# Joined small products per chunk on TensorE and a written-out order in the opening of an attention and two-MoE kernel

## The chip, the cores and the metric

The kernel runs on one core of a Trainium2 chip. Its engines work side by side and wait for each other by semaphores: TensorE multiplies matrices (its products and its weight loads are two rows of a profile, PE and PEld), VectorE (DVE), ScalarE (ACT) and GpSimd (POOL) work on elements, and SyncE (SP) issues most transfers. What counts is the device time of one execution in microseconds, lower is better.

## The reference

A gated linear attention over 4 sequences of 768 tokens (8 heads of 48) feeds a dense gated layer over 3072 tokens, whose result feeds a layer of 8 experts of which each token takes the best one.

```python
f = 1.0 / (1.0 + np.exp(-f_logit))
for t in range(S):
    state = f[:, :, t, :, None] * state + np.einsum('bhd,bhe->bhde', k[:, :, t], v[:, :, t])
    y[:, :, t] = np.einsum('bhd,bhde->bhe', q[:, :, t], state)
...
gate = 1.0 / (1.0 + np.exp(-(x @ w_gate)))
val = x @ w_val
x = gate * val @ w_out
...
logits = x @ moe2_w_gate              # one of 8 experts for a token, by argmax
h = np.maximum(np.einsum('ecd,edf->ecf', disp, w1), 0.0)
out = gate_w * np.einsum('ecf,efd->ecd', h, w2)
```

The weights of the dense layer arrive as 64-bit numbers and are turned into pairs of 32-bit ones (a high and a low part) on the chip.

## The kernel before

The 3072 tokens are 24 chunks of 128. A chunk's attention is done in stages, each a function `s...(i)`: s0a to s0c make the decays (transposes of the gate's logits on TensorE, a tanh on ScalarE, two scans on VectorE), s1 and s1b turn keys and queries and scale them, s2 makes the scores of the eight heads (L425), s2b masks them on VectorE (L435), s3 turns the scaled keys back (L443), s4 makes the chunk's own state, kn times v (L456), and s4b adds it to the state before (`u`, L477). s4a multiplies the state by the decays on GpSimd into `up` (L466), in which a mask leaves only a head's own 48 by 48 block of each pair of heads. The order of chunks is `SEQ`: the first chunks of the first three sequences come first, so chunks 0 to 2 and 18 have no earlier state. Chunks 7, 12, 17 and 23 are the last of their sequences and make no state (no s3, no s4).

The output is made in one of two ways. Chunks 0 to 5 (`SPLIT_FROM` is 6) have s5: tokens on rows, L488 for the earlier state and L496 for the own scores, with v or `up` moving; a copy; and s6 and s6b, which turn the result with TensorE (L517) and split it into xh and xl (L526, L527). Chunks 6 to 23 have s5t: columns on rows, L542 for the scores with v stationary, and L553 for the earlier state, in which each head uses its own rows r of `up` and of the queries. Its result is copied (L565), stored to DRAM by s6t as `xt` (L574), read back as `x` (L576) in the arrangement of the next layer, and split by s6x (L587, L588).

The dense layer goes over 8 blocks of 3 chunks. A block has 12 steps of 27 products with 384 or 392 moving columns: g1 (L756) makes gate and value, g1b the nonlinearity, and g2 (L789) adds into three output banks, which evac copies out after a block's last step. While block n runs, the chunks of block n + 1 are done between its products: `STEPS` says which stage stands in which of eight half-steps of a chunk (for chunks 3 to 5 a list in `chunk`). So chunks 3 to 5 are done in block 0.

Before block 0 stands the opening: the list `EARLY` of stages for chunks 0 to 2 and parts of 3, with `W` for a step of the weights' conversion. Such a step works on several units of weights at once: three VectorE instructions convert one unit (L637, L645, L652), ScalarE and VectorE split the one before (L718, L719), and an output unit is turned on TensorE (L715), copied (L725) and multiplied by the experts' gate (L736). 36 units are converted in all, in the opening and in block 0. In the program before, only SyncE's instructions keep the written order; on the other engines a scheduler moves them ahead of each other by its own estimates. The code around the change that sets the opening's order is this:

```python
for item in EARLY.split():
    if item == "W":
        weights_step()
    else:
        i, stage = item.split(".")
        stages[stage](int(i))
```

Of the kernel before, what the change touches and what calls it, by code (L numbers as in the profile page):

```python
# [8 lines left out]
F32 = mybir.dt.float32  # L9
# [23 lines left out]
STEPS = "s1b s3 +lq;;s2 s2b;s4 s4b;+s0a;s5t +s0b;s6t +s0c *lv +s4a;s6x +s1"  # L33

EARLY = """
0.s0a 0.s0b W 0.s0c W 0.s1 0.s1b W 1.s0a 1.s0b W 0.s3 1.s1 0.s2 0.s4 1.s0c W 2.lq 1.s1b
W 2.s0a 1.s2 0.s2b 2.lv 0.s4b 2.s0b W 0.s5 2.s0c 1.s3 1.s2b W 2.s1 2.s1b 1.s4 1.s4b 2.s3 3.lv 4.lq
1.s5 3.lq W 2.s2 0.s6 0.s6b W 3.s0a 2.s2b 1.s6 3.s0b W 1.s6b 2.s4 2.s4b 2.s5 W 2.s6 4.lv 3.s0c 2.s6b
# [3 lines left out]
EARLY_BANKS = ("a0", "a1", "a2", "acc0", "acc1", "pv")  # L42
# [23 lines left out]
def kernel(  # L66
# [197 lines left out]


# [215 lines left out]

    def s5(i):
        b, c = SEQ[i]
        y = att_bank()
        qt, vt = C[i]["qt"], v_t.pop(i)
        for p in range(NPAIR):
            if c > 0:
                nc.tensor.matmul(  # L488
                    y[:, p * 2 * D : (p + 1) * 2 * D],
                    lhsT=qt[0:PR, p * P : (p + 1) * P],  # L490
                    rhs=C[i]["up"][:, p, :],
                    start=True,
                    stop=False,
                )
            for h in (2 * p, 2 * p + 1):
# [1195 lines left out]
```

## Time and profile before

| what | before |
|---|---|
| device time, median of 3 runs (range) | 888.56 us (887.03 to 888.79) |
| the profiled execution, its time | 888.59 us |
| its span, first to last instruction | 886.8 us |
| TensorE products busy | 856.0 us, 97% |
| TensorE weight loads busy | 814.6 us, 92% |
| VectorE busy | 528.2 us, 60% |
| ScalarE busy | 396.5 us, 45% |
| GpSimd busy | 188.6 us, 21% |
| mean granted clock of TensorE | 0.982 |

A share of busy time is a mean over stages with different limits. The page of the profile also cuts the span into 40 slices: VectorE is nine tenths busy or nearly so in slices 2 to 6 and five to seven tenths in most of those after, and TensorE's granted clock is below full in the first slices alone. So the opening is read apart from the rest, by stretches. TensorE's busy time has a model in it (products overlap and their ends are worked out), so the time of a group of products is read from starts, not from busy times.

### The profile page before, as it was taken

How to read it: one execution, taken by the hardware profiler on the slowest of the kernel's cores; microseconds unless marked ns; L12 is line 12 of the kernel's file. 1: busy time of each engine (PE TensorE's matmuls, PEld its weight loads, DVE VectorE, ACT ScalarE, POOL GpSimd, SP SyncE). 2: the span in 40 equal slices, each digit the busy share in tenths (PEclk: the TensorE clock that was granted, in tenths of full speed). 3: DMA queues.
4: the chain of work that ended last, by engine and by line, in shares of the span. 5: the costliest groups of instructions: out<-in, count | busy, mean ns of one | idle time of the engine just before them, and what ended most of it. 6: DMA issues, size and time to landing. Idle time of an engine off the chain costs nothing.

```text
span 886.8 us, 15168 instructions
## 1 busy us (share of the span) xinstructions
PE 856.0 (97%) x5627; PEld 814.6 (92%) x5627; DVE 528.2 (60%) x1227; ACT 396.5 (45%) x972; POOL 188.6 (21%) x249
## 2 busy tenths in 40 slices
PE   4999999999999999999999999999999999999995
PEld 4889989999999999999999999999899999999995
DVE  5889997756755765665675663353765525644521
ACT  3544433555554554544445454332455525543521
POOL 2032210121111111110110110020274225423311
PEclk8789999999999999999999999999999999999998
DMA  9756543543543533423544441130457235335000
GB/s 224 149 141 154 153 112 82 134 113 96 155 112 78 151 97 99 126 80 105 138 107 108 126 109 54 63 141 21 168 171 249 70 131 195 100 113 172 26 22 25
DMA packets 130245, 103.54 MB, mean 117 GB/s; under 512 B 52056, under 2 KB 123272, under 8 KB 130162
## 3 DMA queue, kind: packets, MB, share of 16 engines
q1 hardware_dynamic: 126546, 93.04, 38.0%
q0 software_dynamic: 3616, 9.44, 3.2%
q8 instruction: 46, 0.75, 0.4%
q14 instruction: 37, 0.30, 0.1%
HBM read 89.95 MB, written 13.46 MB: 117 GB/s over the span
## 4 chain that ended last, share of the span: by engine, by line
PE 79%; DVE 10%; issue 5%; ACT 1%; POOL 1%; DMA 1%; SPq 0%; POOLq 0%; DVEq 0%; ACTq 0%
PE acc L789 16%; PE pv L756 16%; PE pg L756 16%; PE acc L1168 6%; PE pg L1147 5%; PE pv L1147 4%; PE a L425 2%; PE acc L1183 2%; PE a L542 2%; PE a L553 2%; PE a L456 1%; DVE a L652 1%; DVE a L645 1%; PE a L1126 1%; POOL out_dram L1225 1%
## 5 line engine op out<-in xcount | busy, mean ns | idle before, releaser
L768 DVE SCALAR_TENSOR_TENSOR th<-th,pv 128x384 f32<-128x384 f32 x96 | 52.6, 548 | 110.7 <-PE pv L756 109.0
L756 PE MATMUL pg<-xh,wh 128*128 128x384 f32 x288 | 102.3, 355 | 1.2 <-ACT th L766 0.6
L789 PE MATMUL acc<-oh,hh 128*128 128x392 f32 x288 | 101.4, 352 | 0.3 <-ACT x L818 0.3
L789 PE MATMUL acc<-ol,hh 128*128 128x392 f32 x288 | 98.5, 342 | 0.0
L756 PE MATMUL pg<-xl,wh 128*128 128x384 f32 x288 | 97.7, 339 | 0.8 <-DVE xl L527 0.8
L756 PE MATMUL pv<-xh,wh 128*128 128x384 f32 x288 | 97.5, 339 | 0.8 <-DVE th L768 0.7
L756 PE MATMUL pg<-xh,wl 128*128 128x384 f32 x288 | 97.7, 339 | 0.0
L789 PE MATMUL acc<-oh,hl 128*128 128x392 f32 x288 | 97.7, 340 | 0.0
L756 PE MATMUL pv<-xh,wl 128*128 128x384 f32 x288 | 97.0, 337 | 0.0
L756 PE MATMUL pv<-xl,wh 128*128 128x384 f32 x288 | 96.5, 335 | 0.0
L766 ACT ACTIVATE th<-pg 128x384 f32<-128x384 f32 x96 | 47.1, 491 | 100.5 <-PE pg L756 98.2
L773 ACT CAST hh<-th 128x384 fp32r<-128x384 f32 x96 | 49.2, 513 | 94.1 <-DVE th L768 92.3
L466 POOL TENSOR_TENSOR up<-u,gm 112x384 f32<-112x384 f32 x20 | 36.5, 1824 | 213.7 <-PE a L553 189.1
L774 DVE TENSOR_TENSOR hl<-th,hh 128x384 fp32r<-128x384 f32 x96 | 54.0, 562 | 36.8 <-ACT hh L773 36.8
L674 ACT ACTIVATE piece<-piece,tiny 128x192 f32<-128x192 f32 x144 | 67.4, 470 | 17.4 <-DMA piece<-in_moe_w_val_dram 6.3
L756 PEld LDWEIGHTS pg<-xh,wh 128*128 128x128 f32 x288 | 54.4, 189 | 5.4 <-issue 3.3
L789 PEld LDWEIGHTS acc<-oh,hh 128*128 128x128 f32 x288 | 54.0, 188 | 2.8 <-ACT x L818 0.6
L756 PEld LDWEIGHTS pv<-xh,wh 128*128 128x128 f32 x288 | 54.3, 189 | 2.1 <-DVE th L768 1.6
L756 PEld LDWEIGHTS pg<-xl,wh 128*128 128x128 f32 x288 | 54.6, 190 | 1.3 <-DVE xl L527 1.2
L756 PEld LDWEIGHTS pg<-xh,wl 128*128 128x128 f32 x288 | 54.5, 189 | 0.0
L789 PEld LDWEIGHTS acc<-ol,hh 128*128 128x128 f32 x288 | 54.2, 188 | 0.1
L756 PEld LDWEIGHTS pv<-xl,wh 128*128 128x128 f32 x288 | 54.3, 189 | 0.0
(335 smaller groups left out, 2051.2 us busy)
## 6 DMA issues: line engine op xcount, KB each, us to landing
r<-in_moe_w_dram SPq DMA_DIRECT2D x16, 1536.0 KB, 7.6
raw<-in_moe_w_out_dram SPq DMA_DIRECT2D x12, 384.0 KB, 4.0
raw<-in_moe_w_gate_dram SPq DMA_DIRECT2D x12, 384.0 KB, 3.8
raw<-in_moe_w_val_dram SPq DMA_DIRECT2D x12, 384.0 KB, 3.6
v<-in_v_dram SPq DMA_DIRECT2D x24, 192.0 KB, 3.3
x1d<-x SPq DMA_DIRECT2D x24, 192.0 KB, 1.9
piece<-in_moe_w_gate_dram SPq DMA_DIRECT2D x24, 192.0 KB, 3.4
piece<-in_moe_w_val_dram SPq DMA_DIRECT2D x24, 192.0 KB, 3.1
```

The costliest lines, as they stand in the source:

```text
L425: nc.tensor.matmul(pair(sc[hh], p), lhsT=pair(kt, p)[r0 : r0 + D], rhs=pair(qt, p)[r0 : r0 + D], start=True, stop=True)
L466: nc.gpsimd.tensor_tensor(out=up, in0=state[b], in1=gm_t.pop(i)[0:PR], op=ALU.mult)
L542: nc.tensor.matmul(pair(y, p)[64 * z : 64 * z + D], lhsT=vt[:, h * D : (h + 1) * D], rhs=C[i]["a", z][:, p, :], start=(p == 0), stop=(c == ...
L674: nc.scalar.activation(out=words[:, :, 0], in_=words[:, :, 1], func=AF.Sign, bias=tiny[:, z : z + 1], accum_out=above[:, z, n % NF : n % N ...
L756: nc.tensor.matmul(ps[:, 0:nt], lhsT=w[:, kk, :], rhs=x[:, kk, 0:nt], start=(m == 0), stop=(m == len(ops) - 1))
L766: nc.scalar.activation(out=th[:, 0:nt], in_=pg[:, 0:nt], func=AF.Tanh, scale=0.5)
L768: nc.vector.scalar_tensor_tensor(out=g[:, 0:nt], in0=th[:, 0:nt], scalar=1.0, in1=pv[:, 0:nt], op0=ALU.add, op1=ALU.mult)
L773: nc.scalar.copy(out=hh[:, 0:nt], in_=g[:, 0:nt])
L774: nc.vector.tensor_tensor(out=hl[:, 0:nt], in0=g[:, 0:nt], in1=hh[:, 0:nt], op=ALU.subtract)
L789: nc.tensor.matmul(acc[i][:, 0:DE], lhsT=a[:, ts], rhs=w, start=(f == 0 and m == 0), stop=(f == NF - 1 and m == 2),)
L1147: nc.tensor.matmul(ps, lhsT=wt[:, kk, fs], rhs=x[:, kk, c0 : c0 + w], start=(m == 0), stop=(m == len(ops) - 1))
L1168: nc.tensor.matmul(acc[e, d][:, 0 : CAPS[e]], lhsT=w[:, f, d * P : (d + 1) * P], rhs=a[:, 0 : CAPS[e]], start=(f == 0 and m == 0), stop=(f ...
```

## The change

The state group s4 makes two products of a pair of heads in place of one: 64 and 48 stationary columns, 48 moving ones, each to its own half of the result's rows. So only a head's own block is made, `u` is half as large, and `up` is made with all 112 rows of a pair for each head (the mask's zeros stand in the other head's rows). L553's successor takes all these rows. GpSimd makes a second product, `uc`, the decayed state without the mask's zeros, which s4b adds. In `STEPS` s3 moves to the half-step of s2, and s4 and s4b to that of s5t. s5, s6 and s6b are gone: all chunks use s5t, s6t and s6x. s6t is cut in two: it stores, and the new s6i reads back; for chunks 0 to 2 the store is issued by ScalarE. In the opening the instructions of TensorE and ScalarE keep the written order too, `EARLY` is written anew, and `warm` puts products of the identity by itself (256 columns, in bank pv, read by nobody) at the start (12) and at each `X` (8).

```diff
-STEPS = "s1b s3 +lq;;s2 s2b;s4 s4b;+s0a;s5t +s0b;s6t +s0c *lv +s4a;s6x +s1"
+STEPS = "s1b +lq;;s3 s2 s2b;;+s0a;s4 s4b s5t +s0b;s6t s6i +s0c *lv +s4a;s6x +s1"
 EARLY = """
-...
-1.s5 3.lq W 2.s2 0.s6 0.s6b W 3.s0a 2.s2b 1.s6 3.s0b W 1.s6b 2.s4 2.s4b 2.s5 W 2.s6 4.lv 3.s0c 2.s6b
+0.s0a X 0.s0b W 0.s0c 0.s1 X W 0.s1b W 1.s0a X 1.s0b W 0.s3 0.s2 1.s1 0.s4 1.s0c W 2.lq 1.s1b
+W 2.s0a 0.s2b 1.s2 0.s4b 2.s0b W 0.s5t 0.s6t 2.lv 2.s0c 1.s3 1.s2b W 2.s1 2.s1b 1.s4 1.s4b 2.s3 1.s5t 1.s6t 3.lv 4.lq
+3.lq 0.s6i W 2.s2 0.s6x W 3.s0a 2.s2b 3.s0b W 1.s6i 1.s6x 2.s4 2.s4b 2.s5t 2.s6t 4.lv W 3.s0c 2.s6i 2.s6x
 3.s4a
 """
-EARLY_BANKS = ("a0", "a1", "a2", "acc0", "acc1", "pv")
+EARLY_BANKS = ("a0", "a1", "a2", "acc0", "acc1")
+WARM = (12, 8)
...
+    def warm(n):
+        w = ident.bitcast(BF16)
+        for _ in range(n):
+            nc.tensor.matmul(bank("pv")[:, 0 : 2 * P], lhsT=w[:, 0:P], rhs=w, start=True, stop=True)
...
         for p in range(NPAIR):
-            ps = slice(p * 2 * D, (p + 1) * 2 * D)
-            nc.tensor.matmul(
-                kv[0:PR, ps], lhsT=kn[:, p * PR : (p + 1) * PR], rhs=vt[:, ps], start=True, stop=True
-            )
+            for z in range(2):
+                h, n = 2 * p + z, (64, D)[z]
+                nc.tensor.matmul(
+                    kv[64 * z : 64 * z + n, p * D : (p + 1) * D],
+                    lhsT=kn[:, p * PR + 64 * z : p * PR + 64 * z + n],
+                    rhs=vt[:, h * D : (h + 1) * D],
...
-            nc.gpsimd.tensor_tensor(out=up, in0=state[b], in1=gm_t.pop(i)[0:PR], op=ALU.mult)
+            nc.gpsimd.tensor_tensor(
+                out=up,
+                in0=state[b].unsqueeze(2).to_broadcast([PR, NPAIR, 2, D]),
+                in1=gm_t.pop(i)[0:PR].rearrange("p a (z d) -> p a z d", z=2),
+                op=ALU.mult,
+            )
+            uc = atp.tile([PR, NPAIR, D], F32, tag="uc", name="uc")
+            nc.gpsimd.tensor_tensor(
+                out=uc,
+                in0=state[b],
+                in1=e_all[0:PR, i, :].unsqueeze(2).to_broadcast([PR, NPAIR, D]),
+                op=ALU.mult,
+            )
...
-                r = slice(64 * z, 64 * z + D)
                 nc.tensor.matmul(
-                    pair(y, p)[r],
-                    lhsT=C[i]["up"][r, p, z * D : (z + 1) * D],
-                    rhs=pair(qt, p)[r],
+                    pair(y, p)[64 * z : 64 * z + D],
+                    lhsT=C[i]["up"][:, p, z],
+                    rhs=pair(qt, p)[0:PR],
...
-            nc.sync.dma_start(out=rows_[z], in_=t[64 * z : 64 * z + D])
-        x = at2["pool"].tile([P, KD, P], F32, tag="x", name="x", bufs=2)
-        nc.sync.dma_start(out=x, in_=d.rearrange("(k p) t -> p k t", p=P))
+            (nc.scalar if i < len(blocks[0]) else nc.sync).dma_start(out=rows_[z], in_=t[64 * z : 64 * z + D])
+        C[i]["d"] = d
+
+    def s6i(i):
+        if i < len(blocks[0]):
+            x = com.tile([P, KD, P], F32, tag="th", name="x")
...
+        nc.sync.dma_start(out=x, in_=C[i].pop("d").rearrange("(k p) t -> p k t", p=P))
...
+        with tc.manual_schedule(engines={mybir.EngineType.SP, mybir.EngineType.PE, mybir.EngineType.Activation}):
+            warm(WARM[0])
+            for item in EARLY.split():
+                if item == "W":
+                    weights_step()
+                elif item == "X":
+                    warm(WARM[1])
+                else:
+                    i, stage = item.split(".")
+                    stages[stage](int(i))
```

On TensorE, in a chunk of the later blocks, the state group stands between block products before (L456, `kn` and `v` into a bank `a`; L789 and L756 are the block's products):

```order
L789 MATMUL acc_1797<-oh_724,hh 128x392
L789 MATMUL acc_1797<-ol_725,hh 128x392
L789 MATMUL acc_1797<-oh_724,hl 128x392
L456 MATMUL a_2302<-v,kn 112x96 x4
L756 MATMUL pg<-xh,wh_1310 128x384
L756 MATMUL pg<-xl,wh_1310 128x384
```

Of the change, the same engine between the last product into a block's banks (L777) and the next block product (L744):

```order
L777 MATMUL acc_1921<-oh_261,hl 128x392
L466 MATMUL a_1925<-v,kn 64x48
L466 MATMUL a_1925<-v,kn 48x48
...
L522 MATMUL a_1936<-a_1850,v 48x128
L522 MATMUL a_1936<-a_1852,v 48x128
...
L532 MATMUL a_1936<-qt,up 48x128 x8
L744 MATMUL pg<-xh,wh_688 128x384
```

The state group has moved from a place of its own to directly ahead of the output group, and no block product stands between them.

On ScalarE, at the end of the opening, before: `ysb` and `xh` of chunk 2 and what stands around them (`u` is a chunk's state, `oh` and `wh` are the high parts of weights, `wot` the copy of a turned output unit).

```order
L479 COPY u_571<-a2_566 112x384
L718 CAST oh5_550<-a_506 128x384
L725 COPY wot_562<-pg_552 128x384
L505 COPY ysb_582<-acc0_573 128x384
L526 CAST xh_492<-acc1_600 128x3x128
L718 CAST wh7_592<-a_548 128x384
```

Of the change, the same engine from the weight cast ahead of chunk 1's `xh` to chunk 2's `xh` (`t` is chunk 2's output, `xt` its store):

```order
L706 CAST wh8_766<-a_686 128x384
L575 CAST xh_584<-x_648 128x3x128
L506 COPY u_661<-acc1_652 112x192
L545 COPY t_672<-a0_663 48x512 x2
L554 DMA xt_675<-t_672 48x4x128 x2
L706 CAST wh7_688<-a_632 128x384
...
L713 COPY wot_831<-a0_821 128x384
L575 CAST xh_584<-x_702 128x3x128
```

The cast of a weight now stands ahead of chunk 1's `xh`, chunk 2's output goes through two copies and two stores, and its `xh` comes eight rows later.

## Rows read from the trace of the kernel before

**Rows 1.** Busy time by stretch: stretch, length, each engine's us, TensorE's clock, DMA.

```profile
8.10:46.40 38.30, 31.59 (x208) 28.70 (x208) 32.80 (x74) 18.52 (x41) 0.92 (x3) 0.78 0.90 189
53.30:150.30 97.00, 94.48 (x628) 89.61 (x629) 84.71 (x179) 38.33 (x80) 17.99 (x20) 0.98 0.46 121
150.30:560.00 409.70, 409.31 (x2936) 389.26 (x2935) 252.45 (x585) 205.89 (x551) 59.23 (x73) 1.00 0.41 110
```

**Rows 2.** TensorE's waits from 130 to 640: for whom, total us, times, longest.

```profile
PE acc L1183 <- DVE hl L1153: 1.3, 1, 1.3
```

**Rows 3.** Timeline of TensorE from 330 to 370: start, us, line, tiles, shapes, count.

```profile
337.66 0.93 PE L456 MATMUL a<-v,kn 128*112 128x96 f32 x8
...
338.64 0.34 PE L756 MATMUL pg<-xl,wh 128*128 128x384 f32 x1
...
343.04 0.34 PE L789 MATMUL acc<-oh,hl 128*128 128x392 f32 x1
343.30 1.08 PE L542 MATMUL a<-a,v 128*48 128x128 f32 x16
344.31 1.08 PE L553 MATMUL a<-qt,up 48*48 48x128 f32 x16
...
345.60 0.33 PE L756 MATMUL pg<-xl,wh 128*128 128x384 f32 x1
...
353.32 0.55 PE L443 MATMUL a<-ident,kt 112*128 112x112 f32 x4
...
353.90 0.34 PE L789 MATMUL acc<-ol,hh 128*128 128x392 f32 x1
```

**Rows 4.** TensorE's waits from 0 to 160, the two longest.

```profile
PE pg L715 <- DVE a L652: 4.5, 1, 4.5
PE a L344 <- DMA xf<-in_f_logit_dram: 4.1, 1, 4.1
```

**Rows 5.** Timeline of TensorE around chunk 5's output, in block 0.

```profile
129.23 0.36 PE L488 MATMUL a<-up,qt 112*128 112x96 f32 x2
...
132.09 0.33 PE L756 MATMUL pv<-xl,wh 128*128 128x384 f32 x1
...
133.48 0.49 PE L517 MATMUL a<-ident,ysb 128*128 128x128 f32 x3
...
133.99 0.34 PE L789 MATMUL acc<-ol,hh 128*128 128x392 f32 x1
```

**Rows 6.** Timeline of TensorE in the opening, two scores of one pair of heads.

```profile
19.18 0.42 PE L425 MATMUL a<-qt,kt 48*128 48x128 f32 x1
19.22 0.42 PE L425 MATMUL acc<-qt,kt 48*128 48x128 f32 x1
```

**Rows 7.** Timeline at the opening's end: last mask of chunk 2, first block products.

```profile
45.74 0.69 DVE L435 TENSOR_TENSOR a<-acc,mask 128x512 f32<-128x512 f32 x1
...
49.93 0.59 PE L756 MATMUL pg<-xh,wh 128*128 128x384 f32 x1 [0.57 <-ACT xh L526]
...
53.32 0.69 PE L756 MATMUL pg<-xl,wh 128*128 128x384 f32 x1 [0.78 <-DVE xl L527]
```

**Rows 8.** The tiles t and x (ns min/median/max; landing in us), and one issue.

```profile
L565 ACT COPY t<-a x36: 560/582/583, 157.4 to 559.0; 48x512 f32<-48x512 f32 x36
L574 SPq DMA_DIRECT2D xt<-t x36: 309/310/437, 158.0 to 559.6; - x36
DMA to landing us min/median/max: 1.9/1.9/2.1
DMA to landing us min/median/max: 1.8/2.6/4.2
6.55 2.77 SPq L276 DMA_DIRECT2D xk<-in_k_dram  x1
```

**Rows 9.** Timeline of TensorE: four transposes of keys, early and in block 0.

```profile
10.43 1.06 PE L400 MATMUL acc<-ident,xk 128*128 128x128 f32 x4
...
87.82 0.65 PE L400 MATMUL a<-ident,xk 128*128 128x128 f32 x4
```

More of the change, by code (lines that the diff above doesn't have):

```diff
@@ L454, in s4 @@
         for p in range(NPAIR):
-            ps = slice(p * 2 * D, (p + 1) * 2 * D)
-            nc.tensor.matmul(
-                kv[0:PR, ps], lhsT=kn[:, p * PR : (p + 1) * PR], rhs=vt[:, ps], start=True, stop=True
-            )
+            for z in range(2):
[4 more added lines that the diff above has]
+                    rhs=vt[:, h * D : (h + 1) * D],
+                    start=True,
+                    stop=True,
+                )
         C[i]["kv"] = kv
@@ L480, in s4b @@
         state[b] = u
[L482 to L495, printed above, removed]
-                nc.tensor.matmul(
-                    y[:, h * D : (h + 1) * D],
-                    lhsT=C[i]["a", h % 2][:, p, :],
-                    rhs=vt[:, h * D : (h + 1) * D],
-                    start=(c == 0),
-                    stop=(c == 0 or h % 2 == 1),
-                )
-        pool, tag = (com, "th") if i < len(blocks[0]) else (atp, "kn")
-        ysb = pool.tile([P, DM], F32, tag=tag, name="ysb")
-        nc.scalar.copy(out=ysb, in_=y[:, 0:DM])
-        C[i]["ysb"] = ysb
-    def s6(i):
-        n = next(n for n, b in enumerate(blocks) if i in b)
-        j = blocks[n].index(i)
-        if j == 0:
-            xh_t[n] = xp.tile([P, KD, MAXB * P], F32R, tag="xh", name="xh")
-            xl_t[n] = xp.tile([P, KD, MAXB * P], F32R, tag="xl", name="xl")
-        ysb = C[i].pop("ysb")
-        yt = att_bank()
-        for kk in range(KD):
-            nc.tensor.transpose(yt[:, kk * P : (kk + 1) * P], ysb[:, kk * P : (kk + 1) * P], ident)
-        C[i]["yt"] = yt
-    def s6b(i):
-        n = next(n for n, b in enumerate(blocks) if i in b)
-        j = blocks[n].index(i)
-        yt = C[i].pop("yt")
-        src = yt[:, 0:DM].rearrange("p (k t) -> p k t", k=KD)
-        xh, xl = xh_t[n][:, :, j * P : (j + 1) * P], xl_t[n][:, :, j * P : (j + 1) * P]
-        nc.scalar.copy(out=xh, in_=src)
-        nc.vector.tensor_tensor(out=xl, in0=src, in1=xh, op=ALU.subtract)
     at2 = {}
@@ L560, in s5t @@
                 )
-        t = at2["pool"].tile([P, NPAIR, P], F32, tag="t", name="t", bufs=2)
+        pool, bufs = (atp, 1) if i < SPLIT_FROM else (at2["pool"], 2)
+        t = pool.tile([P, NPAIR, P], F32, tag="t", name="t", bufs=bufs)
         src = y.rearrange("p (a t) -> p a t", a=NPAIR)
@@ L1287, in chunk @@
                 [(s0a, n)] if nx else [],
-                [(s2, i), (s2b, i)] + ([(s0b, n)] if nx else []),
-                [(s3, i), (partial(then, load_qk), i)] + ([(s0c, n)] if nx else []),
-                [(s4, i), (s4b, i)],
-                [(s5, i)],
-                [(s6, i), (s6b, i), (load_v, i + 2)],
-                [(s4a, n)] if nx else [],
+                [(s3, i), (s2, i), (s2b, i)] + ([(s0b, n)] if nx else []),
+                [(partial(then, load_qk), i)] + ([(s0c, n)] if nx else []),
+                [(s4, i), (s4b, i), (s5t, i)],
+                [(s6t, i), (load_v, i + 2)],
+                [(s6i, i)],
+                [(s6x, i)] + ([(s4a, n)] if nx else []),
             ]
         stages = dict(s4a=s4a, s0a=s0a, s0b=s0b, s0c=s0c, s1=s1, s1b=s1b, s2=s2, s2b=s2b, s3=s3, s4=s4, s4b=s4b)
-        stages.update(s5t=s5t, s6t=s6t, s6x=s6x, s5=s5, s6=s6, s6b=s6b, lq=load_qk, lv=load_v)
+        stages.update(s5t=s5t, s6t=s6t, s6i=s6i, s6x=s6x, lq=load_qk, lv=load_v)
         plan = {}
```

25 lines of the change are left out of this document (11 added, 14 removed).

## The prediction

> **What bounds the kernel now.** I first read which engine is busy in each stretch. From 150.3 to 560 us TensorE is busy 409.31 of 409.70 us at a clock of 1.00 [rows 1], and between 130 and 640 us its longest wait is 1.3 us [rows 2]. There the kernel is a queue of products, and whatever a chunk's small products take from that queue is time of the kernel, one for one. The opening is different. From 8.1 to 46.4 us, between the first weights' arrival and the end of chunk 2's masks, VectorE works 32.80 of 38.30 us while TensorE runs at a mean clock of 0.78 [rows 1]: VectorE's queue sets the pace, with 5.5 us of waits in it. From 53.3 us, when block 0's products start in earnest, to 150.3 us, when block 0 is evacuated, TensorE is busy 94.48 of 97.00 us [rows 1, 7]. So the change has three terms: the chunks' groups in the steady part, the products of chunks 3 to 5 inside block 0, and the moment at which block 0 starts.
>
> **The steady groups.** One product of 384 columns starts 0.174 us after the one before it, one of 392 columns 0.177 us. What a group takes is the time to the second block product behind it, less those steps. The state group (s4) starts at 337.66 and the second product behind it at 338.64: 0.98 - 0.17 = 0.81 us. The output group (L542 and L553) follows a product that started at 343.04, and the second product behind it starts at 345.60: 2.56 - 0.35 = 2.21 us. The transposes (s3) run from 353.32 to 353.90: 0.58 - 0.18 = 0.40 us [rows 3]. Entering the output group takes 0.26 us instead of 0.18. L542's 16 instructions start 0.054 us apart (its 1.08 us end 0.27 us, one instruction's length, after the last start), so the seventeenth could start at 344.16; L553, which uses other rows of the array, starts at 344.31 [rows 3]. With all 112 rows of `up` the change puts L553's successor on the same half-width columns as L542, so I let this 0.15 us go. The new state group uses those columns too and stands directly ahead. Entering, 16 starts of the state group, 32 of 0.054 and 0.42 to the second block product (344.31 + 16 x 0.054 to 345.60) make 0.26 + 16p + 1.73 + 0.42, less 0.35: 2.06 + 16p us, against 0.81 + 2.21 = 3.02 before.
>
> The price p of one instruction of the new state group stands in no row: there are twice as many, with 64 or 48 stationary columns instead of 112 and 48 moving instead of 96. From above, L542 with 128 moving columns starts every 0.054; from below, two such products that use different halves start 0.04 us apart at the low clock (19.18 and 19.22) [rows 3, 6], and half of 0.054 is 0.027. The old state group's 8 instructions end after 0.93 us, a start each 0.096 us for 112 stationary columns [rows 3], which is 0.048 for a mean of 56. I take 0.048, the row of the same operation. A chunk then takes 2.83 instead of 3.02: 0.19 us less; with 0.027 it is 0.53, with 0.054 0.10.
>
> The Trainium skill (TensorE: Matmul & The Clock Gate, Wait — 56ns, not 53.3ns?) speaks of about 62 ns for every product when its instructions are decoded in the sequencer's code. By that the group would be 16 x 0.062 = 0.99 us, an estimate, and the join would lose 0.03 us a chunk. The starts 0.04 us apart [rows 6] speak against it here.
>
> Transposes and scores (s3, s2) are joined as well. Alone, s3 pays some 0.09 us on its return to block products; joined, the scores wait at s3's end for the array to change its division, about as long. I count nothing, and cover the term by 0 to 0.1. Of chunks 6 to 23, 13 have a state group and an earlier state: 13 x 0.19 = 2.5 us. Four last chunks have no state group and gain the 0.15: 0.6. Chunk 18 gains some 0.15. **Steady term: -3.2 us**, from 0 (a start each 0.06) to -7.7.
>
> GpSimd's new product `uc` is half as large as `up`, and VectorE's sum is halved. Neither is on the path: from one chunk's state to the next chunk's use there are eight half-steps, some 24 us. If that cover were gone, 1 us a chunk would show.
>
> **Chunks 3 to 5.** Their output was made from 129.23 to the second product at 132.09, 2.86 - 0.17 = 2.69 us, and turned by s6 in 133.99 - 133.48 - 0.18 = 0.33 us [rows 5]. With a state group of 0.8 that is 3.8; now 2.8. **-3.0 us** for three chunks, all in the stretch in which TensorE is busy. Their trip through DRAM has half a block to end in.
>
> **The opening.** In the new queue of VectorE eight instructions fewer stand ahead of chunk 2's last mask: one conversion of three, two splits, the first xl, small ones not counted; by 0.55 to 0.4 us each with their overlap some 2.8 us. 32.8 - 2.8 = 30.0 us of work from 8.1: the masks end at 38.1 + s, where s is what VectorE still waits. Before, chunk 2's output, its transposes and xh followed at once, and the first block product came at 49.93, 3.5 us behind the masks' end [rows 7]. Now the way is longer. ScalarE's queue has the cast of a weight (wh8_766) ahead of chunk 2's copies, and this weight's conversion stands 22 instructions behind the mask on VectorE: by their shapes some 8.5 us. Then come the cast, chunk 1's xh and the copy of u, 0.5 us each; two copies of 0.58; two DMA issues of 0.31; 1.9 us to landing; another issue; 2.6 us for x; and xh, 0.5 [rows 8]. These make 1.5 + 1.2 + 0.6 + 1.9 + 0.4 + 2.6 + 0.5 = 8.7 us. Block 0 starts at 38.1 + 8.5 + 8.7 + s = 55.3 + s. For s I take half of the 5.5 us of before, 2.7: the idle-time products and the written order bring chunk 0 forward, but TensorE still has holes and will not keep its clock. **Start at 58.0 instead of 53.3**, between 55.3 and 62 (twice the old half where both queues wait for each other).
>
> The 36 idle-time products cost 256/384 of 0.174, 0.116 us each at the high clock, 0.23 at the low: 4 to 8 us in all, where TensorE waited 4.1 and 4.5 us [rows 4]. That the first transposes ran at the low clock is seen in their time: four took 1.06 us at 10.43 and 0.65 at 87.82 [rows 9]. These eight or nine us are the cover; only the last eight products, 0.9 us, lie ahead of work that is nearly ready.
>
> Block 0 then has less left. Two output-weight units (transposes and gate products), chunk 4's first transposes and half of chunk 3's scores now stand ahead of its first product: 3.7 us by their rows' steps. Chunks 3 to 5 take 3.0 less. VectorE is about two conversions further on, for which I take 1.0 us of waits off. 97.0 - 7.7 = 89.3; 58.0 + 89.3 = 147.3 instead of 150.3. **Opening and chunks 3 to 5 together: -3.0 us**, from -9 (start at 55.3, waits and half clock gone) to +2.
>
> **Sum** against the profiled execution of 888.59 us (a span of 886.8 and 1.8 around it; the median of three is 888.56, so the two agree): -3.2 - 3.0 = -6.2, **882.4 us**. Blocks 1 to 7 and the experts start from block 0's end, and their queue and loads move with it.
>
> **Rivals.**
> 1. *ScalarE and the DRAM trip set the start (slower).* Chunk 2's two stores are issued on ScalarE's queue, in written order ahead of two casts and chunk 4's decay. One issue on SP took 2.77 us at 6.55 us, when transfers were queued, and x took up to 4.2 [rows 8]. At such prices the way from the copies grows by 2 x 2.5 + 1.6 + 2 = 8.6 us, for an issue that stalls, x and a late landing of the stores; VectorE then waits for xl. With s = 5.5 the start is 69, and block 0's end 158: +8 - 3 = 893.6 us. It decides from a start of about 65 on. For it: transfers share the time with weights there. Against it: the same stores take 1.9 us in the steady part.
> The Trainium skill (DMA: Bandwidth & Descriptors, Issuing engines are not separate DMA queues) says that another issuing engine saves issue time only, since all share 16 engines; that leaves this rival its landing.
> 2. *No gain in either place.* A start each 0.06 us and a beginning at 62: block 0 ends at 151.3, +1.0, and the groups give 0: 889.5, within 0.2%. This is also what it gives if the idle-time products don't hold the clock and the groups still change the array's division at each step.
> 3. *Everything at its good end.* p = 0.027, start at 55.3, fewer waits: -7.5 - 8 = 873 us. VectorE's 30 us speak for it; TensorE's holes speak against.
>
> **How the numbers follow.** Forecast 0.50 (own range 878 to 886), rival 1 0.17, rival 2 0.17, rival 3 0.16. 0.2% (1.8 us) is about what a measurement of this kernel can tell from no change. Faster holds the forecast, rival 3, and little of rival 2: 0.67. Same is most of rival 2 and an edge of the forecast: 0.16; slower is rival 1: 0.17. The range takes rivals 2 and 3 in and cuts off the worse part of rival 1: 872 to 892.
>
> **What would show it.** In the new profile: state group and outputs as one group of about 2.8 us from entry to return, with no wait of the weight load between L522 and L532; the first block product near 58 us and the evacuation of block 0 near 147; VectorE's waits up to chunk 2's masks near 3 us; ScalarE's wh cast just ahead of chunk 1's xh. It is wrong if block 0 starts after 62, if the joined group takes 3 us, or if a wait of TensorE appears in the steady part, where there was none.

## The result and the profile after

The changed kernel takes 897.78 us (896.26 to 897.93), beside 888.67 us (887.03 to 888.83) for the kernel before: a ratio of 1.0104 with a 95% interval of 1.0088 to 1.0120, some 9.1 us slower. The forecast of 882.4 us was wrong in sign, and the time lies above its range. The profiled execution has a span of 895.9 us, 9.1 more than the 886.8 of before, so it shows the whole loss.

To place the loss I use one mark that both traces have: the first product of a block's token routing on TensorE (`oh` by `tri`), which follows each block's evacuation. The first of them, done while block 1 runs, is called block 1's mark or just the mark. 396 products of the dense layer stand ahead of it in both kernels, so by then both have done the same work. The rows of the first and the last one in the timeline of TensorE (start, duration), for the kernel before and then for the changed one:

```profile
159.66 0.18 PE L852 MATMUL a<-oh,tri 128*128 128x8 bf16 x1
...
633.72 0.18 PE L852 MATMUL a<-oh,tri 128*128 128x8 bf16 x1
```

```profile
175.75 0.18 PE L840 MATMUL a<-oh,tri 128*128 128x8 bf16 x1
...
642.76 0.18 PE L840 MATMUL a<-oh,tri 128*128 128x8 bf16 x1
```

Up to the first mark the change lost 16.1 us. From the first mark to the last it gained: 474.06 us before, 467.01 after, 7.05 less. Behind the last mark both take the same (253.1 and 253.2 us). So the steady part gained over twice the forecast's 3.2 us, and the opening lost 16.1 where a gain of 3.0 was forecast.

The stretches of the changed kernel that answer to [rows 1] (columns: stretch, length, busy time and instructions of TensorE, its weight loads, VectorE, ScalarE, GpSimd; granted clock; DMA share, GB/s; the clock of the first row is read too high, as the first experiment shows):

```profile
8.10:46.40 38.30, 33.20 (x210) 23.84 (x208) 29.76 (x65) 16.27 (x34) 1.41 (x3) 0.87 0.70 161
46.40:76.20 29.80, 18.56 (x102) 15.20 (x103) 19.65 (x44) 10.88 (x24) 8.40 (x18) 0.54 0.69 164
76.20:160.50 84.30, 80.75 (x594) 76.91 (x593) 72.77 (x156) 36.17 (x73) 16.46 (x15) 0.96 0.51 137
160.50:560.00 399.50, 399.50 (x3019) 385.70 (x3018) 253.81 (x587) 203.03 (x550) 72.61 (x91) 1.00 0.42 113
```

From 46.4 to 76.2 us no engine is the bound: TensorE works 18.56 of 29.80 us, VectorE 19.65, ScalarE 10.88. This stretch hardly existed before: block 0's products began at 49.93 us [rows 7], and here the first comes at 76.20. ScalarE's timeline there (in brackets the idle time before a row, and what ended it) shows two of the waits that fill it; the last rows are TensorE's:

```profile
45.83 0.48 ACT L713 COPY wot<-pg 128x384 f32<-128x384 f32 x1
54.25 0.51 ACT L575 CAST xh<-x 128x384 fp32r<-128x384 f32 x1 [7.94 <-DMA x<-xt]
...
64.66 0.51 ACT L706 CAST wh<-a 128x384 fp32r<-128x384 f32 x1 [6.36 <-DVE a L640]
...
65.70 1.18 ACT L545 COPY t<-a 48x512 f32<-48x512 f32 x2
66.31 0.91 ACTq L554 DMA_DIRECT2D xt<-t  x2
...
74.00 0.51 ACT L575 CAST xh<-x 128x384 fp32r<-128x384 f32 x1
```

```profile
52.61 1.08 PE L408 MATMUL a<-ident,xk 128*128 128x128 f32 x4 [4.60 <-DMA xk<-in_k_dram]
55.60 1.45 PE L724 MATMUL acc<-wg,wot 128*128 128x8 f32 x6 [1.91 <-ACT wot L713]
```

Chunk 0's x holds ScalarE for 7.94 us, with the casts and copies of two weights (wot) behind it, for which TensorE and VectorE wait in turn. The weight's cast holds it for 6.36 us, with chunk 2's copies (t) behind it. Then chunk 2's trip takes from 65.70 to 74.00. Chunk 0's x was late because its load stands on SP behind four loads for chunks 3 and 4, of which the issue of one took 2.12 us; and from its issue to ScalarE's start it then took 4.7 us (49.55 to 54.25), where the median of such loads is 2.5 to landing. Ahead of those four SP had stood some 8.3 us, up to 43.86, at a weight's load that waits for VectorE. TensorE waits for these loads too: 4.60 us for keys (xk). SP's timeline:

```profile
43.86 0.37 SPq L592 DMA_DIRECT2D raw<-in_moe_w_val_dram  x1
...
44.85 0.53 SPq L284 DMA_DIRECT2D xk<-in_k_dram  x1
45.49 2.12 SPq L284 DMA_DIRECT2D xq<-in_q_dram  x1
...
48.70 0.80 SPq L284 DMA_DIRECT2D xq<-in_q_dram  x1
49.55 1.09 SPq L564 DMA_DIRECT2D x<-xt  x1
```

At the beginning of the trace the idle-time products stand in front of the small ones (first the group of line 271, with shortest/median/longest duration in ns, then TensorE's timeline):

```profile
L271 PE MATMUL pv<-ident x36: 370/370/421, 1.5 to 22.0; 128*128 128x256 bf16 x36
```

```profile
1.54 5.09 PE L271 MATMUL pv<-ident 128*128 128x256 bf16 x12 [1.54 <-POOL ident L217]
6.43 1.06 PE L352 MATMUL a<-ident,xf 128*128 128x128 f32 x4
7.28 3.40 PE L271 MATMUL pv<-ident 128*128 128x256 bf16 x8
```

Twelve took 5.09 us and eight 3.40: 0.425 us each, 15.3 us for 36 (5.09 + 3 x 3.40), where the forecast had 4 to 8 us.

### The profile page after: what moved, and what is told of

It reads as the page before. It is cut to its first block, busy times and chain, and to the rows that moved or that the text cites. A ratio compares the mean times of both kernels' runs of the same rounds, so it can differ in the third digit from the quotient of the medians.

```text
span 895.9 us, 15639 instructions
## 1 busy us (share of the span) xinstructions
PE 860.9 (96%) x5829; PEld 814.2 (91%) x5829; DVE 529.7 (59%) x1227; ACT 399.0 (45%) x978; POOL 205.2 (23%) x269
## 3 DMA queue, kind: packets, MB, share of 16 engines
q1 hardware_dynamic: 130194, 94.81, 38.1%
## 4 chain that ended last, share of the span: by engine, by line
PE 84%; DVE 6%; issue 5%; ACT 2%; POOL 1%; DMA 1%; SPq 0%; POOLq 0%; DVEq 0%; ACTq 0%
PE pg L744 17%; PE acc L777 17%; PE pv L744 16%; PE acc L1156 6%; PE pg L1135 5%; PE pv L1135 5%; PE a L433 3%; PE a L522 2%; PE acc L1171 2%; PE a L532 2%; PE pv L271 1%; PE a L466 1%; PE a L1114 1%; POOL out_dram L1213 1%; PE a L1171 1%
## 5 line engine op out<-in xcount | busy, mean ns | idle before, releaser
L756 DVE SCALAR_TENSOR_TENSOR th<-th,pv 128x384 f32<-128x384 f32 x96 | 52.6, 548 | 112.3 <-PE pv L744 109.4
L744 PE MATMUL pg<-xh,wh 128*128 128x384 f32 x288 | 101.4, 352 | 1.4 <-ACT xh L575 1.4
L777 PE MATMUL acc<-oh,hh 128*128 128x392 f32 x288 | 101.3, 352 | 0.0
L777 PE MATMUL acc<-ol,hh 128*128 128x392 f32 x288 | 99.1, 344 | 0.0
L777 PE MATMUL acc<-oh,hl 128*128 128x392 f32 x288 | 98.4, 342 | 0.0
L744 PE MATMUL pg<-xh,wl 128*128 128x384 f32 x288 | 97.6, 339 | 0.0
L744 PE MATMUL pg<-xl,wh 128*128 128x384 f32 x288 | 97.3, 338 | 0.0
L744 PE MATMUL pv<-xh,wl 128*128 128x384 f32 x288 | 96.6, 335 | 0.0
L744 PE MATMUL pv<-xh,wh 128*128 128x384 f32 x288 | 96.4, 335 | 0.0
L744 PE MATMUL pv<-xl,wh 128*128 128x384 f32 x288 | 96.2, 334 | 0.0
L744 PEld LDWEIGHTS pg<-xh,wh 128*128 128x128 f32 x288 | 54.6, 189 | 5.0 <-issue 3.3
L777 PEld LDWEIGHTS acc<-oh,hh 128*128 128x128 f32 x288 | 54.4, 189 | 2.8 <-issue 0.4
L1090 POOL DMA_INDIRECT xg<-x1d,idx x30 | 34.5, 1150 | 91.1 <-PE a L1114 61.7
L777 PEld LDWEIGHTS acc<-ol,hh 128*128 128x128 f32 x288 | 54.7, 190 | 0.2 <-issue 0.2
L744 PEld LDWEIGHTS pg<-xl,wh 128*128 128x128 f32 x288 | 54.6, 190 | 0.0
L777 PEld LDWEIGHTS acc<-oh,hl 128*128 128x128 f32 x288 | 54.4, 189 | 0.2
L744 PEld LDWEIGHTS pg<-xh,wl 128*128 128x128 f32 x288 | 54.4, 189 | 0.0
L744 PEld LDWEIGHTS pv<-xh,wh 128*128 128x128 f32 x288 | 54.2, 188 | 0.0
```

Source lines behind the costliest of these rows:

```text
L744: nc.tensor.matmul(ps[:, 0:nt], lhsT=w[:, kk, :], rhs=x[:, kk, 0:nt], start=(m == 0), stop=(m == len(ops) - 1))
L756: nc.vector.scalar_tensor_tensor(out=g[:, 0:nt], in0=th[:, 0:nt], scalar=1.0, in1=pv[:, 0:nt], op0=ALU.add, op1=ALU.mult)
L777: nc.tensor.matmul(acc[i][:, 0:DE], lhsT=a[:, ts], rhs=w, start=(f == 0 and m == 0), stop=(f == NF - 1 and m == 2),)
L1090: nc.gpsimd.indirect_dma_start(out=xg[0:n, j, :], out_offset=None, in_=x1d[0:top, :], in_offset=bass.IndirectOffsetOnAxis(ap=col, axis=0), ...
```

## Experiments

All marks below are block 1's first routing product, as above. Times are medians, beside the kernel before on the same chip (888.2 to 888.8 us).

**The idle-time products.** Taken out, and then put in so that none waits for the one before:

```diff
-WARM = (12, 8)
+WARM = (0, 0)
```

> The changed kernel without its 36 idle-time products. In its trace they took 15.3 us of TensorE (0.425 us each), and the first transposes began at 6.43 us instead of 4.13. Theory A (ScalarE's two waits in written order, 7.9 us for chunk 0's x and 6.4 us for a weight, set block 0's start): the start moves by only 1 to 3 us, 895 to 897 us. Rival B (the idle-time products are what delays the opening): the start moves by 5.6 us or more, the lateness of chunk 0's first transposes, 892 us or less. Rival C (they hold the granted clock, as they are written for): the clock from 8 to 46 us falls from 0.87 to the 0.78 of the kernel before and the time stays at 898 or grows to 900.

890.72 us, ratio 1.0013 (0.9990 to 1.0037); mark 168.86 us, 6.9 earlier; first block product at 69.31. That is Rival B. My Theory A was wrong: the waits on ScalarE didn't hide these products, the whole chain moved with them (chunk 2's last mask ends at 40.52 instead of 46.84 us). ScalarE's two long waits are still there, 7.2 and 6.4 us. Rival C is wrong, though its figures seem to say otherwise: from 8.1 to 46.4 us the row of the stretch has a clock of 0.67 without these products, where it had 0.87:

```profile
8.10:46.40 38.30, 25.95 (x195) 21.29 (x195) 31.69 (x71) 14.33 (x30) 1.37 (x3) 0.67 0.95 203
```

But such a row counts as full clock all time ahead of the trace's first record of the clock, and in the changed kernel the first record, of the full clock, stands at 28.1 us. Until then TensorE ran at the low one: four transposes still took 1.06 us at 26.00, as those of [rows 9] did at the low clock, and only from 28 on were they faster (the changed kernel's stretches and TensorE's timeline):

```profile
8.10:28.10 20.00, 18.30 (x89) 11.72 (x88) 15.76 (x33) 7.29 (x15) 0.86 (x2) 1.00 0.80 188
28.10:46.40 18.30, 14.90 (x122) 12.12 (x122) 13.99 (x32) 8.99 (x19) 0.55 (x1) 0.72 0.60 132
```

```profile
26.00 1.06 PE L410 MATMUL acc<-ident,xq 128*128 128x128 f32 x4
...
47.41 0.60 PE L352 MATMUL acc<-ident,xf 128*128 128x128 f32 x4
```

With half clock up to 28.1 and 0.72 behind it, the mean from 8.1 to 46.4 us is 0.61, an estimate: less than without these products, not more. Their first full clock comes at 28.1 us; without them it comes at 7.6, and in the kernel before at 12.5. So they didn't raise the clock, although TensorE counts as busy for 18.30 of the 20.00 us; and VectorE, which works 31.69 us here instead of 29.76, got further without them.

```diff
+        pv = bank("pv")
-        for _ in range(n):
-            nc.tensor.matmul(bank("pv")[...], lhsT=w[:, 0:P], rhs=w, start=True, stop=True)
+        for k in range(n):
+            nc.tensor.matmul(pv[...], lhsT=w[:, 0:P], rhs=w, start=(k == 0), stop=(k == n - 1))
```

> The changed kernel with each row of idle-time products summed up in one bank instead of each product beginning the bank anew, so that none of them waits for the one before it to be out. Theory (the 0.425 us of each is the wait for the product before it, not its columns): 0.23 us each or less at the low clock, 12 in some 2.6 us instead of 5.09 and 36 in 8 us or less instead of 15.3, the start of block 0 some 3 to 5 us earlier than 76.2, 893 to 895 us. Rival (0.425 us is what such a product takes at the low clock): the same 5.09 us, 897 to 898 us.

892.21 us, ratio 1.0035 (1.0025 to 1.0045); mark 169.40, first block product at 69.65. The timeline of TensorE:

```profile
1.54 2.74 PE L272 MATMUL pv<-ident 128*128 128x256 bf16 x12 [1.54 <-POOL ident L217]
4.09 0.96 PE L353 MATMUL a<-ident,xf 128*128 128x128 f32 x4
4.89 1.04 PE L272 MATMUL pv<-ident 128*128 128x256 bf16 x8
```

0.23 us each in the row of twelve at 1.2 GHz, and 0.13 each in the row of eight at 2.4 GHz (the first record of the full clock stands at 4.8 us): the forecast's two prices within 0.02. The other 0.2 us was a wait for the product before, and the start comes 6.6 us earlier than 76.20, more than the 3 to 5 expected. In the mark 6.35 of the 6.9 us come back, so nearly all of the loss was these waits (and the low clock that came with them), and the products without them buy nothing: masks end at 40.34, beside 40.52 with none.

**ScalarE's written order.** Chunk 0's and chunk 1's xh behind chunk 2's copies, and one more weight step inside the list:

```diff
-3.lq 0.s6i W 2.s2 0.s6x W 3.s0a 2.s2b 3.s0b W 1.s6i 1.s6x 2.s4 2.s4b 2.s5t 2.s6t 4.lv W 3.s0c 2.s6i 2.s6x
+3.lq 0.s6i W 2.s2 W 3.s0a 2.s2b 3.s0b W 1.s6i 2.s4 2.s4b 2.s5t 2.s6t 0.s6x 1.s6x 4.lv W 3.s0c 2.s6i W 2.s6x
```

> The changed kernel with two casts moved in the written list: chunk 0's and chunk 1's xh behind chunk 2's two copies and stores, and one more weight step inside the list, so that no weight's cast stands ahead of these copies. Theory A (ScalarE's two waits set the start): both waits go from ahead of chunk 2's copies, the copies start near 56 instead of 65.70 us, block 0 near 67 instead of 77.2, and the time is 886 to 890 us. Rival (TensorE's late small products or the loads set the start, and ScalarE only waited in their shadow): the copies move by less than 3 us, 895 to 898 us.

892.74 us, ratio 1.0038 (1.0012 to 1.0064); mark 169.49, 6.3 earlier. The copies start at 55.20 and block 0 at 63.38, both earlier than Theory A asked, but of these 12.8 us only half arrives at the mark: from the first block product to the mark it is 106.1 us, beside 99.6 in the changed kernel. TensorE has small products left that it would have done while waiting: with the same 396 block products, 29 groups of small ones stand between them up to the mark, beside 17. The mechanism holds; the size I gave to it (8 to 12 us) doesn't.

The same by leaving ScalarE's order to the scheduler:

```diff
-engines={mybir.EngineType.SP, mybir.EngineType.PE, mybir.EngineType.Activation}
+engines={mybir.EngineType.SP, mybir.EngineType.PE}
```

> The changed kernel with TensorE and SP in written order and ScalarE's order left to the scheduler, which puts chunk 0's xh behind chunk 2's copies too, and the next weight's cast behind them. Theory A: as with the two casts moved by hand, 886 to 891 us. Rival (the written order of TensorE, not of ScalarE, is what holds the opening): 895 to 898 us.

890.98 us, ratio 1.0013 (0.9985 to 1.0041); mark 169.71: about the same gain, 6.0 us, by the other way, though block 0 starts at 68.74 here.

Both edits together, no idle-time products and the casts moved:

> The changed kernel with both edits: no idle-time products, and the two casts moved behind chunk 2's copies with one more weight step in the list. In their own traces the first edit brought the first routing product of block 1 from 175.75 to 168.86 us, the second to 169.49. Theory (two separate causes): they add up, 175.75 - 6.9 - 6.3 = 162.6, a span of about 882.7 and 885 us as a time. Rival (they overlap: what delays the opening by the one is hidden in the wait of the other): about 167, 888 to 890 us. What is left over 159.66, the mark of the kernel before, is then the trip through DRAM and the written order of TensorE.

887.14 us, ratio 0.9979 (0.9967 to 0.9992); mark 164.12. Of 13.2 us 11.6 add up: two causes with a small overlap. What is left shows as one hole on TensorE, which waits for chunk 2's trip; its timeline and then ScalarE's:

```profile
57.29 0.69 PE L744 MATMUL pg<-xh,wh 128*128 128x384 f32 x1 [7.99 <-ACT xh L575]
```

```profile
47.97 1.18 ACT L545 COPY t<-a 48x512 f32<-48x512 f32 x2 [1.39 <-PE a L522]
48.58 1.00 ACTq L554 DMA_DIRECT2D xt<-t  x2
...
56.73 0.51 ACT L575 CAST xh<-x 128x384 fp32r<-128x384 f32 x1 [1.76 <-DMA x<-xt]
```

From t to xh 8.76 us.

**The trip taken out.** The changed kernel's list in written order on all three engines, but chunks 0 to 2 turned on TensorE (the old functions s5, s6 and s6b put back), and no idle-time products. The bank pv is also given back to the opening's small results, as in the kernel before (`EARLY_BANKS` has six banks again); so it is in all versions below with outputs turned on TensorE but the last:

```diff
-... 0.s5t 0.s6t ... 0.s6i W 2.s2 0.s6x ... 2.s5t 2.s6t 4.lv W 3.s0c 2.s6i 2.s6x
+... 0.s5 ... 0.s6 W 2.s2 0.s6b ... 2.s5 4.lv W 3.s0c 2.s6 2.s6b
```

> The changed kernel's list, in written order on SP, TensorE and ScalarE, without idle-time products, but the outputs of chunks 0 to 2 turned on TensorE as in the kernel before, with no trip through DRAM. Everything behind the opening is the changed kernel's. Theory A (the trip and the waits that it puts into ScalarE's queue are the cost): block 0 starts near 51 us as in the kernel before, the routing mark is near 159.7, and the time is 880 to 883 us. Rival B (the written order is itself a cost, whatever it orders): a start of 56 us or later, routing mark 164 or more, 886 us or more.

882.84 us, ratio 0.9938 (0.9924 to 0.9953); mark 158.54, first block product at 50.70. Theory A. ScalarE:

```profile
47.20 0.48 ACT L532 COPY ysb<-acc 128x384 f32<-128x384 f32 x1 [1.14 <-PE acc L523]
...
50.17 0.47 ACT L553 CAST xh<-acc 128x384 fp32r<-128x384 f32 x1
```

2.97 us from the output's copy to xh, where the trip took 8.76. So the new list in written order costs nothing that these marks show (158.54, beside 159.69 for the old list below), and the opening's loss splits, mark by mark, into: idle-time products 175.75 - 168.86 = 6.9; the trip 168.86 - 158.54 = 10.3, of which 4.7 goes with the two waits on ScalarE's queue, for x and for the weight's cast (168.86 - 164.12), and 5.6 with the trip itself, half clock during the waits included; and 158.54 - 159.66 = -1.1 for the rest. What the sixth bank adds isn't separated: it stands inside the 5.6. Each mark is that of one execution.

**The joined groups alone.** The kernel before with its own opening, and joined groups and the trip from chunk 3 on:

> The opening of the kernel before (chunks 0 to 2 with their outputs turned on TensorE, the old list, SP alone in written order, no idle-time products), with the joined groups and the trip through DRAM for chunks 3 to 23. Theory (the groups gain 13 x 0.47 us and some 0.9 in the others, and chunks 3 to 5 1.27 us each, as the two traces show): -7.0 - 3.8, 877.9 us. Rival 1 (chunks 3 to 5 give nothing, since VectorE or the trip takes it back before block 1): 881.7 us. Rival 2 (the steady gain in the trace of the changed kernel was catching up after a late start): 887 to 889 us.

883.05 us, ratio 0.9924 (0.9896 to 0.9952); mark 159.69, span 880.2. Nearest is Rival 1: the steady gain is there in full (from the first to the last mark 467.04 us), and chunks 3 to 5 give nothing. TensorE's timeline at the border of block 1 suggests why:

```profile
141.40 0.42 PE L569 MATMUL a<-a,v 128*48 128x128 f32 x2 [0.65 <-DVE a L443]
142.70 0.67 PE L791 MATMUL pg<-xh,wh 128*128 128x384 f32 x1 [0.88 <-ACT xh L622]
143.16 0.52 PE L791 MATMUL pv<-xh,wh 128*128 128x384 f32 x1
143.61 1.10 PE L569 MATMUL a<-a,v 128*48 128x128 f32 x8
```

Block 1's first product waits for an xh that came by way of DRAM, and chunk 5's group is torn into pieces around it. After these holes products take 0.52 us instead of 0.34.

**What in the group is cheaper.** The state products in their old form, directly ahead of the output (only their diagonal blocks are read, and s4b sums them in two instructions), on top of the version with the trip taken out:

```diff
-                    kv[64 * z : 64 * z + n, p * D : (p + 1) * D],
-                    lhsT=kn[:, p * PR + 64 * z : p * PR + 64 * z + n],
-                    rhs=vt[:, h * D : (h + 1) * D],
+                kv[0:PR, ps], lhsT=kn[:, p * PR : (p + 1) * PR], rhs=vt[:, ps],
```

> The version with the changed kernel's list and the outputs of chunks 0 to 2 turned on TensorE, but the state products in the old form: 8 full-width products of 96 columns each instead of 16 half-width ones of 48, still directly ahead of the output group (only their diagonal blocks are then read). Theory (the steady gain is that two half-width state products run beside each other, a start each 0.028 us, and change the array's division once): the joined group takes 2.8 us or more instead of 2.54, and blocks 1 to 7 take 3 to 4 us more than the 467.05 us from the first to the last routing mark. Rival (the place next to the outputs is the gain, whatever the form): 2.54 us, 467 us.

889.86 us, ratio 0.9996 (0.9968 to 1.0025); its opening came out otherwise (mark 165.28), so only what follows is read: 471.09 us from the first to the last mark (636.37 - 165.28), 4.0 more than 467.05. Its group, and the changed kernel's:

```profile
204.39 0.34 PE L821 MATMUL acc<-oh,hl 128*128 128x392 f32 x1
204.57 0.93 PE L465 MATMUL a<-v,kn 128*112 128x96 f32 x8
...
207.60 0.34 PE L788 MATMUL pg<-xl,wh 128*128 128x384 f32 x1
```

```profile
332.07 0.34 PE L777 MATMUL acc<-oh,hl 128*128 128x392 f32 x1
332.33 0.61 PE L466 MATMUL a<-v,kn 128*64 128x48 f32 x15
332.73 0.30 PE L522 MATMUL a<-a,v 128*48 128x128 f32 x1
332.77 0.22 PE L466 MATMUL a<-v,kn 128*64 128x48 f32 x1
332.83 1.04 PE L522 MATMUL a<-a,v 128*48 128x128 f32 x15
333.63 1.11 PE L532 MATMUL a<-qt,up 112*48 112x128 f32 x16
334.68 0.44 PE L744 MATMUL pg<-xh,wh 128*128 128x384 f32 x1
334.96 0.33 PE L744 MATMUL pg<-xl,wh 128*128 128x384 f32 x1
```

207.60 - 204.39 - 0.35 = 2.86 us with the old state products, 334.96 - 332.07 - 0.35 = 2.54 with the new; 3.02 before. The place next to the outputs gives 0.16 us, the form 0.32. Over 13 chunks 0.32 makes 4.2 us, which fits the 4.0.

**A version that beats both.** Chunk 5's output turned on TensorE too, first in the old opening, then in the list with the trip taken out:

```diff
+            if i in (5,):
+                return [..., [(s4, i), (s4b, i)], [(s5, i)], [(s6, i), (s6b, i), (load_v, i + 2)], ...]
```

> The opening of the kernel before with joined groups and the trip through DRAM from chunk 6 on and for chunks 3 and 4, while chunk 5, whose output block 1 needs first, has its output turned on TensorE as in the kernel before. In the trace with chunk 5 joined, TensorE had holes at 139 to 143 us in front of block 1 and then ran at half its clock from 142.7 to 146.2 us. Theory (chunk 5's trip is too late for block 1's start and costs what chunks 3 to 5 save): the routing mark comes 2 to 4 us earlier than 159.69, 878 to 880 us by the kernel before's 888.6. Rival (VectorE's weights set block 0's end, and TensorE's saving there is worth nothing): 159.7 again, 881.7 us.

881.57 us (879.22 to 886.01), ratio 0.9916 (0.9899 to 0.9933). Its profiled execution took 886.01 us, the longest of six, with half clock from 27.7 to 61.8 us that the version with chunk 5 joined didn't have (0.76 there), so its mark (163.55) doesn't answer the question.

> The version with the changed kernel's list in written order and the outputs of chunks 0 to 2 turned on TensorE (routing mark 158.54 us, span 881.5), with chunk 5's output turned on TensorE too, so that block 1's first operand doesn't come by way of DRAM. Theory (the waits of 0.7 and 0.9 us at 140 to 143 us and the half clock from 142.4 to 145.8 us come from that trip): both go, the routing mark comes near 156, 879 to 880.5 us. Rival (something else holds the end of block 0): 158.5 again, 882.8 us.

880.70 us (879.87 to 881.43), ratio 0.9904 (0.9871 to 0.9937): the lowest median of all, 888.16 - 880.70 = 7.5 us faster than the kernel before on its chip; from the two versions next to it, 0.9916 and 0.9938, its ratio is not clear by the intervals. The mark comes at 157.09, 1.45 us earlier than with chunk 5 by way of DRAM (2.5 were expected), block 1's wait is gone, and the clock stays at 2.4 GHz from 139 to 148 us (0.50 from 142.4 to 145.8 before).

> The same version with the outputs of chunks 3, 4 and 5 all in the old form, turned on TensorE; only chunks 6 to 23 have joined groups. Theory (joined groups save chunks 3 to 5 1.27 us each of TensorE's time, and TensorE is what block 0 waits for): routing mark 1.5 to 3 us later than with chunk 5 alone in the old form, 881 to 883 us. Rival (TensorE's time in block 0 isn't what counts, VectorE's weights are): the same mark within 0.5 us.

884.09 us (880.80 to 888.23), ratio 0.9954 (0.9927 to 0.9981); mark 162.27. This doesn't settle what chunks 3 and 4 gain: its profiled execution had two stretches at 1.2 GHz in the opening (50.4 to 57.3 and 77.8 to 84.6 us) that the version with chunk 5 alone hadn't; the first of them, in this kernel and then in that one:

```profile
50.40:57.30 6.90, 6.11 (x18) 5.60 (x19) 5.42 (x12) 1.64 (x4) 2.78 (x9) 0.51 0.67 169
```

```profile
50.40:57.30 6.90, 5.33 (x30) 4.46 (x30) 6.90 (x15) 2.80 (x7) 2.94 (x9) 1.00 0.62 166
```

**The idle-time products in the good opening.** One bank a row, chunks 0 to 2 turned on TensorE. Bank pv goes to these products, so the opening has five banks for its small results instead of six:

> The version with the outputs of chunks 0 to 2 turned on TensorE, with the 36 idle-time products put back, each row summed up in one bank. Theory (VectorE paces the opening, and the granted clock is worth little there): start of block 0 within 0.7 us of 50.70 or later, 882 to 884 us. Rival (they keep the clock, and TensorE's small products then finish earlier): chunk 2's masks end 1 us or more earlier than 44.1, 880 to 881.5 us.

890.05 us (881.85 to 891.55), ratio 0.9986 (0.9956 to 1.0016). By the median neither: worse than both. But the times fall into two groups: four of ten executions took 881.85 to 885.68 us, at a mean clock of 0.975 to 0.983, and six took 889.95 to 891.55, at 0.966 to 0.973. The profiled one (890.92) is of the second group. Its chunk 2's masks end at 48.79 and its mark is at 166.54, with TensorE at 1.2 GHz from 21.3 to 58.9 us although it is busy 34.04 of 37.60 us. The version without these products, with its sixth bank (second row), has a clock of 0.82 there:

```profile
21.30:58.90 37.60, 34.04 (x192) 31.36 (x191) 26.92 (x61) 13.59 (x31) 5.62 (x13) 0.50 0.61 140
```

```profile
21.30:58.90 37.60, 31.99 (x233) 28.66 (x233) 33.60 (x75) 16.12 (x37) 7.27 (x17) 0.82 0.72 161
```

So these products gain nothing that can be relied on, and don't fix where the stretches of full clock fall. Whether the loss comes from them or from the missing bank isn't separated.

## Why the prediction was wrong, step by step

**Steady groups: right mechanism, size too small.** The working said 2.83 us for the joined group, with p = 0.048 us for a state product from the old operation's row; it is 2.54. The new products start from 332.33 on, and the fifteenth at 332.33 + 0.61 less one product's length of 0.22, 332.72: 0.39 / 14 = 0.028 us, the lower bound that I had named and set aside, since each pair uses the two halves of the columns. The gain is 0.48 a chunk, and 7.05 us in all instead of 3.2 (the bound was 7.7). The 0.15 us of the last chunks' outputs measured 0.13 (2.21 to 2.08). Transposes and scores together gained 0.03 us, inside the 0 to 0.1. No wait of TensorE appeared between 160 and 640 us, and `uc` and VectorE's sum were covered, as said.

On the floor of small products the Trainium skill (TensorE: Matmul & The Clock Gate, Wait — 56ns, not 53.3ns?) gives, beside the 62 ns weighed in the prediction, a start each 25 ns or more whatever the decode; the mean of 0.028 us excludes the first here and lies just above the second. Single starts are closer than that: the first two of this group stand 0.006 us apart (332.332 and 332.338), one on each half of the columns.

**Idle-time products: the term that failed first.** The price 0.12 to 0.23 us stands in the one-bank run (0.13 and 0.23); but each product of the kernel began the same bank anew and waited for the one before, 0.425 us. I counted columns and didn't look for a wait between instructions that write the same tile; in the trace each of them waits on a semaphore that the one before it sets, and inside a row of the one-bank run none does. And the cover was wrong: the old waits of 4.1 and 4.5 us [rows 4] are no cover for 15.3 us, and even less for a row of 5 us ahead of the very first transposes. Cost: 6.9 us. Nor did they hold the clock: full clock came first at 28.1 us, beside 12.5 before.
The Trainium skill (TensorE: Matmul & The Clock Gate, Single matmul latency) gives (219 + N) / 1.2 ns for a product that stands alone at the low clock, 396 ns for 256 columns; the 0.425 us here comes near it. For products in a row the Trainium skill (the same page, Back-to-back issue gap) gives N / 1.2, 213 ns; the 0.23 us of the one-bank run, its last product's end counted in, agrees with that.

**VectorE's waits up to the masks.** s was taken as 2.7 us, between 0 and 5.5; it was 8.7 (46.84 - 38.1). Without the idle-time products the masks end at 40.52, so s is 2.4 then: the step was right, and fell with the one above. VectorE's work was sized well: 30.20 us from 8.1 to the masks' end at 46.84, beside 30.0. The clock of 0.78 [rows 1] that the prediction starts from is read too high, as above: the first record of before stands at 12.5 us, so with half clock up to there it is 0.72, an estimate. The argument doesn't hang on it.

**From the masks to block 0: the largest miss.** 17.2 us were forecast, 29.4 passed (46.84 to 76.20). The weight's cast ahead of chunk 2's copies was foreseen and priced at 8.5 us behind the masks; it came 17.8 behind them (64.66 - 46.84), and this is most of the miss. What I left out: chunk 0's xh stands in ScalarE's written order in the middle of the weights, and its load on SP behind chunk 3's and 4's loads. I priced the trip only for chunk 2, the last, and not as a wait in front of everything that ScalarE does behind it. VectorE then waited 5.9 us for it (xl), and TensorE 1.9 for a weight's copy (wot). The rest of the way took 11.5 us instead of 8.7 (64.66 to 76.20). Of it the trip, from the start of t to the start of xh, is 8.30 us, beside 6.7 in the forecast (8.7 less 1.5 ahead of t and 0.5 for xh); at its end xh waits in ScalarE's queue and not for its x.

**Block 0's remaining work: right for a wrong reason.** I took 7.7 us off. From the first block product to the mark it is 99.55 us in the changed kernel, beside 109.73 before (from 49.93; 106.34 from 53.32). My base mixed the two: the way led to the first product, 49.93 before, and was set against 53.3. So the 7.7 came near by luck (106.34 - 99.55 = 6.8): the versions that start at 50.7 and 50.8 need 107.8 and 106.3 again. The work was shorter in the changed kernel because its small products were done while block 0 waited. Of the 3.0 us for chunks 3 to 5 little arrives: their trip does not have "half a block to end in": chunk 5's ends at block 1's border, and with chunk 5 turned on TensorE the mark comes 1.45 us earlier. What chunks 3 and 4 are worth stays open.

**Rivals.** Rival 1 (the trip and ScalarE's queue set the start, 893.6 us) was the right side and nearly the right place, but not by its price: chunk 2's two issues on ScalarE took 0.91 us, not 2 x 2.5. It decided "from a start of about 65 on", and the start was 76.2. In it I had put a wait for the landing, not the queue behind a wait. Rivals 2 and 3 each had one half: the opening gained nothing, and the price of a state product was the lower bound.

## What to carry to other kernels

When a step goes through DRAM, look up which instruction waits for it, on which in-order queue it stands, and price everything that is behind it, for every chunk and not the last one alone: here the two waits on ScalarE's queue cost 4.7 us, and what was left of the trip 5.6, with the bank that wasn't separated. Work that is put into idle time has to be free of waits on itself and shorter than the hole it is put into; write it to one open accumulation, and measure it alone. Check a clock read from a stretch against the times of known products in it. Small products of one half-width form, put in a row and in pairs on the two halves of the columns, are worth their work: with the place next to the outputs they gained 7 us, and with the old outputs of chunks 0 to 2 and 5 they make the kernel 0.96% faster than before.

## What the runs showed of the hardware

- Two products that use different halves of the columns start 0.028 us apart on average (48 moving columns, 64 and 48 stationary), beside 0.096 for the full-width form of twice the columns [rows 3].
- A product that begins the same bank anew, and that the program therefore lets wait for the one before, takes 0.425 us instead of 0.23 for 256 columns at 1.2 GHz.
- In the changed kernel, with 36 products that wait for one another, full clock was first granted at 28.1 us, although TensorE counts as busy 18.30 of the 20.00 us ahead of it; without these products it came at 7.6 us, with the same ones in open accumulations at 4.8. In another order of the opening TensorE stood 37.6 us at 1.2 GHz while busy 34.04 of them. What decides it isn't settled by these runs.
- Two DMA issues on ScalarE took 0.91 to 1.00 us in most rows, where one on SP had taken 2.77 early in the trace of before [rows 8]; but two of ScalarE's own took 2.97 us in the version with the casts moved (at 43.21), so the engine alone doesn't set the price.
